# Seven half-size products for the last half of W_o, and a new order of the first loads, in a fused adaLN / linear attention / GEGLU block

## The chip, the cores and the metric

One NeuronCore of one Trainium2 chip. The metric is the device time of one execution in microseconds (us); the kernel before takes 749.21 us (median of 3 runs, 748.36 to 750.71). "TensorE" is the matmul engine (PE in the profile), "VectorE" DVE, "ScalarE" ACT, "GpSimd" POOL, and "the queue of transfers" is SyncE's (SP).

## The reference, cut to what matters

```python
# S = 2048 rows, D = 1024, F = 3584, 32 heads of 32; all inputs bf16
def _A_ref(x, wqkv, wo):                      # linear attention
    ...
    o = num / den
    return (lambda x, *d: x.transpose(*d))(o, 0, 2, 1, 3).reshape(B, S, D) @ wo
def _B_ref(x, w_gate, w_up, w_down):
    return _gelu(x @ w_gate) * (x @ w_up) @ w_down
mod = (_silu(c) @ w_mod).reshape(c.shape[0], 6, 1, -1)
sa, ca, ga, sb, cb, gb = ...
h = _layernorm(x, axis=-1) * (1 + ca) + sa
x = x + ga * _A_ref(h, A_wqkv, A_wo)
h = _layernorm(x, axis=-1) * (1 + cb) + sb
x = x + gb * _B_ref(h, B_w_gate, B_w_up, B_w_down)
```

The kernel folds the attention state into W_o (W' = KV · W_o · ga), so that the W_o stage is one product of 2048 x 1024 by 1024 x 1024. The other large products (Q, K, V, gate, up, down) already use seven half-size products in place of eight (Strassen's scheme, in Winograd's form).

## The kernel before: what the change and the argument touch

Every operation is recorded in a plan. A list scheduler then sets the order of the instructions of VectorE, ScalarE, GpSimd and the queue of transfers from modelled times; TensorE keeps the order of the program. So any change of the program lets the scheduler reorder the other four queues in all of the kernel.

```python
    def order(self):                      # (cut)
        best = None
        def forward(look):
            nonlocal best
            t = self.sweep(False, lambda o: (o.due, o.n), look)
            if best is None or t < best[0]:
                best = (t, sorted((op.start, op.n) for op in self.ops))
        ...
        return [self.ops[n] for _, n in best[1]]
```

```python
    def wo_tile(tt, banks):               # one of 16 tiles of 128 rows: 16 matmuls of 512 columns
        b, tl = tt // TT, tt % TT
        xt = x2_ring()
        ...
        for half in range(NHD):
            for g in range(KD):
                te.matmul(psw[:, half, :], lhsT=pqT[b][:, g, tl * P:(tl + 1) * P],
                          rhs=Wp[:, g, half * NW:(half + 1) * NW], start=(g == 0), stop=(g == KD - 1))
        tt_op(xt, psw.rearrange("p h n -> p (h n)"), xt, ALU.add)
        sy.dma_start(out=x2_scr[b][tl * P:(tl + 1) * P, :], in_=xt)

    xh2_ring = Ring(199, [D], F16, 3)     # three slots for the normalised rows on their way to DRAM

    def ln2_xhat(tt, x2, mv, rstd, op0=ALU.subtract):
        xh = xh2_ring()
        ve.tensor_scalar(out=xh, in0=x2, scalar1=mv[:, 0:1], scalar2=rstd[:, 0:1], op0=op0, op1=ALU.mult)
        sy.dma_start(out=xh_scr[g][h][tl * P:(tl + 1) * P, :], in_=xh)
        if tl == TT - 1:
            h2_load(g, h)                 # transposed load of four tiles: the rows of gate/up

    def wo_phase(ms2):
        for tt in range(NTT):             # 16 tiles
            ...
            if tt == NTT - 2:
                ms2.spread(2, gbrow, 1.0)
            if tt < 2 * TT:               # statistics of the first eight tiles, ScalarE or VectorE
                ...
```

The first eight tiles (row blocks 0 and 1) feed the first gate/up stage through normalisation, a store, a transposed load, modulation ("h2_mod") and differences ("h2_t1" and so on). Row blocks 2 and 3 are normalised later.

Terms used below: PSUM is the memory that matmuls write into; SBUF holds the other tiles. The "spread" is two matmuls that copy the gate row of the modulation to all partitions, and the "shift row" is another row of the modulation, wanted at the start. The "denominators" ("den") are the divisors of the attention; they come back from DRAM in the W_o stage. A "seed copy" is a copy by ScalarE from one PSUM bank to another in gate/up, on which TensorE then goes on adding. Names such as s1, s2, t1 or t2 are sums of sub-blocks (s of rows, t of weights) that the seven products take as operands.

## Time and profile before

| | before |
|---|---|
| time, median | 749.21 us |
| span of the profiled run | 746.4 us |
| TensorE busy | 730.0 us, 98% |
| W_o stage, first tile after the denominators to gate/up | 194.75 to 245.6 us |
| VectorE busy from 195 to 250 us | 39.03 of 55 us |
| first gate/up stage | 245.6 to 414.5 us |

The profile is one execution. A group line gives start, length, engine, source line, operation, operands and count; a bracket gives the idle time of the engine just before and what ended it. The prediction shows the summary, the chain, VectorE at three spots and the start. One view more, TensorE in the first gate/up stage (244 to 420 us): these are all its lines with an idle time.

```profile
321.99 4.48 PE L1382 MATMUL psum<-mem 128*128 128x512 f16 x20 [0.31 <-ACT psum L1436]
358.61 4.48 PE L1382 MATMUL psum<-mem 128*128 128x512 f16 x20 [0.16 <-ACT psum L1436]
381.88 0.38 PE L1393 MATMUL psum<-mem 128*128 128x256 f16 x2 [0.42 <-DVE psum L564]
```

Together 0.9 us in 169.

### The profile page before, as it was taken

How to read it: one execution, taken by the hardware profiler on the slowest of the kernel's cores; microseconds unless marked ns; L12 is line 12 of the kernel's file. 1: busy time of each engine (PE TensorE's matmuls, PEld its weight loads, DVE VectorE, ACT ScalarE, POOL GpSimd, SP SyncE). 2: the span in 40 equal slices, each digit the busy share in tenths (PEclk: the TensorE clock that was granted, in tenths of full speed). 3: DMA queues.
4: the chain of work that ended last, by engine and by line, in shares of the span. 5: the costliest groups of instructions: out<-in, count | busy, mean ns of one | idle time of the engine just before them, and what ended most of it. 6: DMA issues, size and time to landing. Idle time of an engine off the chain costs nothing.

```text
span 746.4 us, 11439 instructions
## 1 busy us (share of the span) xinstructions
PE 730.0 (98%) x4164; PEld 388.7 (52%) x4164; DVE 589.5 (79%) x1258; ACT 433.0 (58%) x757; POOL 95.8 (13%) x164
## 2 busy tenths in 40 slices
PE   5999999999999999999999999999999999999997
PEld 2444445444444455545454586545555555548664
DVE  6897997577786878777997888678888888888763
ACT  3665576669752768997876234027777777731000
POOL 2331245000001113342311000010000000000000
PEclk9999999999999999999999999999999999999999
DMA  8974479828899979899659799654131322399822
GB/s 298 322 212 132 152 182 163 299 101 258 245 290 257 364 253 261 259 318 227 187 191 237 210 281 314 206 183 132 60 114 57 112 73 98 110 276 302 278 104 71
DMA packets 151832, 152.79 MB, mean 205 GB/s; under 512 B 33824, under 2 KB 128544, under 8 KB 150496
## 3 DMA queue, kind: packets, MB, share of 16 engines
q1 hardware_dynamic: 128832, 122.44, 53.7%
q0 software_dynamic: 20592, 27.53, 15.6%
q10 hardware_dynamic: 2352, 2.10, 0.8%
q8 instruction: 32, 0.52, 0.3%
q14 instruction: 24, 0.20, 0.1%
HBM read 123.34 MB, written 36.04 MB: 214 GB/s over the span
## 4 chain that ended last, share of the span: by engine, by line
PE 84%; DVE 6%; ACT 5%; DMA 3%; issue 1%; SPq 1%; ACTq 0%; DVEq 0%
PE psum L1382 30%; PE psum L1588 13%; PE psum L1632 9%; PE psum L870 8%; PE psum L1393 7%; PE psum L1262 7%; PE psum L940 5%; DVE mem L564 5%; PE psum L969 4%; DMA mem<-in_A_wqkv_dram 2%; DMA mem<-in_w_mod_dram 1%; PE psum L984 1%; ACT mem L815 1%; DVE psum L564 1%; ACT psum L1436 1%
## 5 line engine op out<-in xcount | busy, mean ns | idle before, releaser
L564 DVE TENSOR_TENSOR mem<-mem 128x512 f16<-128x512 f16 (+8 forms) x669 | 307.8, 507 | 23.1 <-ACT mem L815 10.1
L1382 PE MATMUL psum<-mem 128*128 128x512 f16 x1248 | 299.1, 379 | 0.8 <-ACT psum L1436 0.5
L815 ACT ACTIVATE mem<-psum 128x256 f32<-128x256 f32 (+3 forms) x284 | 154.3, 562 | 119.9 <-PE psum L1382 45.1
L564 DVE TENSOR_TENSOR mem<-psum,mem 128x512 f16<-128x512 f32 (+4 forms) x204 | 155.4, 767 | 72.8 <-ACT mem L815 29.5
L1382 PEld LDWEIGHTS <-mem 128*128 128x128 f16 (+1 forms) x1248 | 122.0, 98 | 112.1 <-issue 2.7
L1588 PE MATMUL psum<-mem 128*128 128x512 f16 (+2 forms) x462 | 99.2, 373 | 0.5 <-DVE mem L564 0.5
L1393 PE MATMUL psum<-mem 128*128 128x256 f16 x560 | 89.5, 272 | 1.3 <-DVE psum L564 1.2
L1393 PEld LDWEIGHTS <-mem 128*128 128x128 f16 (+1 forms) x560 | 54.7, 98 | 46.8 <-issue 5.1
L1588 PEld LDWEIGHTS <-mem 128*128 128x128 f16 x462 | 45.2, 98 | 49.8 <-issue 0.7
L1632 PE MATMUL psum<-mem 128*128 128x256 f16 (+1 forms) x588 | 66.2, 273 | 0.0
L870 PE MATMUL psum<-mem 128*128 128x512 f16 (+1 forms) x280 | 62.9, 379 | 0.0
L1632 PEld LDWEIGHTS <-mem 128*128 128x128 f16 x588 | 57.5, 98 | 9.2
L1436 ACT ACTIVATE psum<-psum 128x512 f32<-128x512 f32 x56 | 32.8, 587 | 41.3 <-PE psum L1382 28.9
L1262 PE MATMUL psum<-mem 128*128 128x512 f16 x256 | 56.0, 379 | 0.0
L940 PE MATMUL psum<-mem 128*128 128x512 f16 x224 | 51.2, 379 | 0.0
L564 DVE TENSOR_TENSOR psum<-psum,mem 128x256 f32<-128x256 f32 x80 | 34.3, 429 | 17.7 <-ACT mem L815 17.3
L870 PEld LDWEIGHTS <-mem 128*128 128x128 f16 x280 | 26.9, 97 | 31.8 <-DVE mem L789 1.2
L1262 PEld LDWEIGHTS <-mem 128*128 128x128 bf16 x256 | 24.8, 98 | 30.3 <-issue 0.8
L1453 ACT ACTIVATE mem<-psum 128x512 f16<-128x512 f32 x56 | 33.1, 595 | 10.9 <-PE psum L1382 10.5
L1463 ACT ACTIVATE mem<-mem 128x512 f16<-128x512 f16 x56 | 34.9, 625 | 1.5 <-DVE mem L564 1.1
L940 PEld LDWEIGHTS <-mem 128*128 128x128 f16 (+1 forms) x224 | 21.5, 98 | 27.0 <-issue 2.0
L1049 POOL DMA_DIRECT2D ts<-in_B_w_down_dram x28 | 28.3, 1199 | 9.2 <-DMA ts<-in_B_w_down_dram 8.9
(132 smaller groups left out, 525.3 us busy)
## 6 DMA issues: line engine op xcount, KB each, us to landing
mem<-in_B_w_gate_dram SPq DMA_DIRECT2D x14, 1024.0 KB, 7.0
mem<-in_B_w_up_dram SPq DMA_DIRECT2D x14, 1024.0 KB, 5.4
mem<-in_w_mod_dram SPq DMA_DIRECT2D x24, 512.0 KB, 5.9
mem<-ts SPq DMA_DIRECT2D x6, 1792.0 KB, 6.8
mem<-in_A_x_dram SPq DMA_DIRECT2D x32, 256.0 KB, 7.7
ts<-in_B_w_down_dram POOLq DMA_DIRECT2D x28, 256.0 KB, 6.3
mem<-ub SPq DMA_DIRECT2D x16, 448.0 KB, 6.7
mem<-in_B_w_down_dram SPq DMA_DIRECT2D x12, 448.0 KB, 7.8
```

The costliest lines, as they stand in the source:

```text
L564: ve.tensor_tensor(out=out, in0=a, in1=b, op=op)
L815: ac.activation(out=t, in_=ps, func=AF.Copy)
L870: te.matmul(ps, lhsT=A[:, k, i * P:(i + 1) * P], rhs=B[:, k, :], start=(start and k == 0), stop=(k == KH - 1), skip_group_check=True)
L940: te.matmul(o, lhsT=W[:, k, (j0 + i) * P:(j0 + i + 1) * P], rhs=h_form(a, k), start=(start and k == 0), stop=(k == KH - 1), skip_group_che ...
L1262: te.matmul(psw[:, half, :], lhsT=pqT[b][:, g, tl * P:(tl + 1) * P], rhs=Wp[:, g, half * NW:(half + 1) * NW], start=(g == 0), stop=(g == K ...
L1382: te.matmul(ps, lhsT=a[:, k, e, :], rhs=b[:, k, :], start=(start and k == 0), stop=(k == KH - 1), skip_group_check=True)
L1393: te.matmul(ps, lhsT=self.x[a][:, k, :], rhs=self.y[y][:, k, :], start=(start and k == 0), stop=(k == KH // 2 - 1), skip_group_check=True)
L1436: ac.activation(out=z, in_=x, func=AF.Copy)
L1453: ac.activation(out=o, in_=ps, func=AF.Gelu_apprx_tanh)
L1463: ac.activation(out=o, in_=o, func=AF.Gelu_apprx_tanh)
L1588: te.matmul(psm[:, q, c], lhsT=A[:, i, q * P:(q + 1) * P], rhs=wt[:, i, c], start=(start and i == 0), stop=(i == NPR - 1), skip_group_chec ...
L1632: te.matmul(ps[:, q, :], lhsT=a[:, k, q * P:(q + 1) * P], rhs=y[:, k, :], start=(start and q == 0 and k == 0), stop=(k == NPR // 2 - 1), s ...
```

## The change

Its intent: W_o of row blocks 2 and 3 costs seven half-size products a block in place of eight (112 matmuls for 128), with the sums of W' and of the rows made on VectorE meanwhile. At the start, the first loads come in the order in which the first products want them, W_v in quarters, so that the first V product can begin sooner.

```diff
+    WpT = [at(11.75 + 4 * i, [KH, NW], F16) for i in range(4)]
+    x2_pair = [at(o, [2, D], BF16) for o in (191, 195, 176, 180)]
...
+    START_LOADS = "c a0 x0 a1 x1 a2 a3 v0 x2 v1 x3 v2".split()
...
-        load_w(Wv[:, 0:KH, 0:NW], 2 * D, NW, 0, KH)
-        load_w(Wv[:, KH:KD, 0:NW], 2 * D, NW, KH, KD)
-        load_w(Wv[:, :, NW:D], 2 * D + NW, NW)
-        plan.chain.append(plan.ops[-1])
+        for name, c in (("v0", slice(0, HB)), ("v1", slice(HB, NW)), ("v2", slice(NW, D))):
+            load_w(Wv[:, :, c], 2 * D + c.start, c.stop - c.start)
+            loads[name] = plan.ops[-1]
+        plan.chain += [loads[name] for name in START_LOADS]
...
-            xh.append(ln_rows(x))
+            xh.append(ln_rows(x, i in (2,3,)))          # statistics of two tiles on ScalarE
...
-        for tt in range(NTT):
+        for tt in range(2 * TT):                        # eight tiles only
...
             if tt == 2:
                 den_sums(1, psX())
+                for i in range(4):
+                    wp_sum(i)
             if tt == 6:
                 ms2.columns()
                 ve.tensor_scalar_add(out=opcB, in0=modT[:, 4 * KD:5 * KD], scalar1=1.0)
+                ms2.spread(2, gbrow, 1.0)
...
+            if tt == 2 * TT - 1:
+                for b in (2, 3):
+                    for i in range(4):
+                        h_sum(b, i, pqT)
+                stages = {2: wo_stages(2, QC, QD)}
+                stages[2][0]()                          # product (2,1), ahead of tile 7
...
+    ORDER = ((2, 3), (2, 2), (3, 1), (2, 5), (3, 3), (2, 4), (3, 2), (2, 6), (3, 5), (2, 7), (3, 4), (3, 6), (3, 7))
+    def wo_stages(b, A, B):
+        ...
+        def s1():
+            st["a"] = products(A.pair(), "a11", "b11", True)
+            st["c"] = B.pair()
+            ac.activation(out=st["c"], in_=st["a"], func=AF.Copy)
+        def s3():
+            st["u2"] = fcopy(lambda: u2 if b == 2 else p1, products(st["a"], "s2", "t2", False))
```

Product (b, j) is number j of row block b. The change also edits some hints to the scheduler (how early the loads of the denominators and the transposed loads are placed).

## The prediction

> **What bounds the kernel now.** I read the engine summary first, then the chain of work that ended last, then the stretches of the two places that the change touches: the first 36 us, and the product with W_o from 195 to 250 us.
>
> ```profile
> PE 730.0 (98%) x4164; PEld 388.7 (52%) x4164; DVE 589.5 (79%) x1258; ACT 433.0 (58%) x757; POOL 95.8 (13%) x164
> ...
> PE 84%; DVE 6%; ACT 5%; DMA 3%; issue 1%; SPq 1%; ACTq 0%; DVEq 0%
> ```
>
> TensorE is busy in 730.0 of 746.4 us and carries 84% of the chain. So a matmul taken away is worth its own time, provided that no new wait opens beside it. The chain, in order of time, in the W_o stage:
>
> ```profile
> 194.81 7.01 PE psum L1262 x32
> ...
> 210.68 0.08 PE psum L592 x4
> 210.76 31.10 PE psum L1262 x144
> 241.86 0.43 PE psum L600 x2
> 242.29 3.45 PE psum L1262 x16
> 245.75 8.63 PE psum L1382 x40
> ```
>
> L1262 is the product with W_o, L600 the spread of the gate row, L1382 the gate/up stage. 31.10 / 144 gives 0.216 us a matmul with 512 columns, and the stages follow each other with no gap. VectorE is not idle here, though:
>
> ```profile
> 195.00:250.00 55.00, 55.00 (x283) 24.86 (x282) 39.03 (x60) 29.34 (x58) 1.87 (x3) 1.00 1.00 277
> ```
>
> After the length come PE, PEld, DVE, ACT and POOL: DVE 39.03 of 55 us. The timeline of VectorE at three spots of this stage:
>
> ```profile
> 197.41 2.50 DVE L564 TENSOR_TENSOR mem<-mem 128x1024 bf16<-128x1024 bf16 x4 [2.12 <-DMA mem<-den]
> 199.82 1.22 DVE L564 TENSOR_TENSOR mem<-psum,mem 128x1024 bf16<-128x1024 f32 x1
> ...
> 216.47 0.17 DVE L594 COPY mem<-psum 128x16 f32<-128x16 f32 x1
> ...
> 244.15 1.39 DVE L564 TENSOR_TENSOR mem<-mem 128x1024 f16<-128x1024 f16 x2 [3.40 <-ACT mem L1240]
> 245.79 1.23 DVE L564 TENSOR_TENSOR mem<-psum,mem 128x1024 bf16<-128x1024 f32 x1 [0.24 <-PE psum L1262]
> ```
>
> The first two lines give the prices: 1024 elements from SBUF 0.63 us each (2.50 / 4), a W_o tile added out of PSUM 1.22 (1.14 from start to start). The pair at 244.15 makes h2_t1, the first difference that gate/up needs; it is done 1.8 us before gate/up's ninth matmul wants it (245.6 + 8 x 0.216 = 247.3). At the start:
>
> ```profile
> 26.50 0.83 PE L636 MATMUL psum<-mem 128*32 128x512 bf16 x12
> 28.07 0.40 PE L636 MATMUL psum<-mem 128*32 128x512 bf16 x4 [0.73 <-DMA mem<-in_w_mod_dram]
> 28.40 0.82 PE L691 MATMUL psum<-mem 128*128 128x512 f16 x3
> ...
> 12.00:19.00 7.00, 5.72 (x34) 2.16 (x32) 3.98 (x13) 1.58 (x4) 0.00 (x0) 1.00 1.09 359
> 20.00:26.00 6.00, 6.00 (x30) 2.70 (x29) 5.37 (x15) 2.65 (x5) 2.24 (x6) 1.00 1.05 385
> ```
>
> TensorE has done all that precedes the shift row of the modulation (L636) by 27.3 us and waits for the last quarter of that row's weights until 28.07. The last two numbers of the stretches say why: the 16 DMA engines are full (1.09, 1.05), at 359 and 385 GB/s. The start is bound by bytes, not by the order of the first products.
>
> [...] ScalarE stood 13.5 us behind the spread of L600 while later work was ready. My two stalls below rest on it. [...] W_v in quarters has rows of exactly 512 B. No run before shows that size.
>
> **The change, part by part.** *Matmuls removed.* Row blocks 2 and 3 took 8 tiles x 16 = 128 matmuls. Seven products take 2 blocks x 7 x 2 row halves x 4 = 112. Gain 16 x 0.216 = 3.45 us. The instruction count of TensorE stays at 4164: two W_v tiles at the start are now made in column halves, 32 matmuls of 256 for 16 of 512, the same column time. So it can't be read from the count.
>
> *Work added, VectorE.* Four sums of W' of 2048 elements (about 1.16 us each, an estimate from the 0.63 us pieces: 4.6), eight row sums of 1024 (8 x 0.60 = 4.8), four second adds of the outputs (2.4). The adds out of PSUM stay at four a block. Together 11.8 us: DVE goes from 39 of 55 to about 51 of 52. ScalarE gets six copies of 1024 (about 1.0 each), 35 of 52: room. Sums of rows, and the division by the denominator ahead of them, are done in time by my count (the second sum of block 3 at about 227, where its product starts at 226.8).
>
> *A stall at the spread.* In the order of the built program the gate row's spread moved from before the last W_o tile to before tile 6. Its second matmul writes the bank that VectorE's 16-column copy (L594 above) reads, so TensorE must wait for that copy. VectorE's queue ahead of it, from the landing of block 1's denominators at 197.4: four multiplies 2.4, tiles 0 and 2 2.3, two W' sums 2.3, tile 3 1.1, a W' sum 1.2, row copy 0.6, two normalisations 0.9, statistics 1.2, tile 4 1.1, a statistic and a normalisation 0.6, two multiplies 1.3, the copy 0.2: 15.2 us, so 212.6. TensorE is there at 210.97. That is 1.7 us if the denominators land when they did. Fewer bytes stand ahead of them in the new order of loads, so they may land 1 to 3 us sooner and the stall may go. I take 0.8.
>
> *A stall at gate/up.* Call T the end of the last W_o product. Before, h2_t1 was placed ahead of the last tile's add. In the changed program VectorE's queue has the last product's add first, then a small sum, three modulations, then h2_t1. From T: [...] 1.14 the add, 0.3, 3 x 0.365, 0.6 for the first half: T + 3.25. TensorE has eight matmuls without it (T + 1.73), so it waits 1.5 us, and about 0.2 more for the second half, whose modulation ScalarE makes after the seed copy (T + 3.0, sum at T + 3.8). I take 1.7. After that VectorE is ahead again.
>
> *The start.* Both orders put the same 8.4 MB (x, W_v, two modulation rows, the next x tiles) ahead of the last shift-row quarter. So the quarter lands when it did, whatever the first products do: opcA about 1.4 us sooner (0.5 MB less ahead of it), first V matmul near 14.1 instead of 15.03, all of it waiting again at 28. The two 512 B quarters may cost bytes per second: 359 at 1 KB rows and 385 at 2 KB rows fit about 6 ns a row plus 39.5 ns per KB on each of 16 engines; 512 B would then run near 316 GB/s, 1.05 MB in 3.3 instead of 2.9 us, +0.4. Interleaving large loads with the small x loads may fill the thin stretch from 2 to 6 us (244 GB/s) and give as much back. Net 0.
>
> Sum: -3.45 + 0.8 + 1.7 + 0 = -0.95; 749.21 - 0.95 = 748.3.
>
> **The rivals.** (a) The full saving, 745.8: TensorE is 98% busy and the chain holds nothing else in this stage. Against it: VectorE has 1 us of slack left in 52, and its order puts h2_t1 behind an add that can't start before T. (b) VectorE becomes the bound of the whole W_o stage; a load that waits behind it (the denominators, the transposed rows) makes it worse; 750 to 751. For it: 51 of 52. Against it: it waits for products anyway from 230 on. The second transposed load, issued at about 228, lands near 239 with the 10 us that the former needed, some 4 us before VectorE asks. (c) The start pays too, 1 us from the earlier first product: 747.3, with (a) 744.8. Against it stands the wait at 28.07. (d) The scheduler reshuffles VectorE and ScalarE everywhere: TensorE's order is the same elsewhere and it waits little there; +-0.7 us.
>
> **Range and chances.** Each stall may be 0 to 2.5 us, the start -0.8 to +0.8, the reshuffle +-0.7. All for the better gives about 744.5, all for the worse 751.5; 745.6 to 750.4 should hold 8 times in 10. Two per cent are 15 us, more than four times the matmuls removed: within 2% 0.98, 0.01 on either side.
>
> **What would show it.** In the changed trace: 16 matmuls fewer between the two stages at 0.216; an idle time of TensorE at the second spread matmul near 211, ended by VectorE (0 to 2 us); one after eight gate/up matmuls, ended by VectorE, of 1.5 to 2; TensorE waiting for the last shift-row quarter at 27.6 to 28.6. I am wrong if gate/up runs through its first 40 matmuls as before, if the last quarter lands more than 1 us sooner, or if new waits show in stages that the change does not touch.

Cut from it: one term of 0.1 us in the stall at gate/up, for the step from the last product's end to VectorE's start, which the trace does not show: before, the add started at 245.79, 0.04 us after the modelled end of the product at 245.75. T + 3.25 counts that term; without it the terms come to T + 3.14 and that wait to 1.4 us in place of 1.5. The forecast was made with it, and its sum stays: -3.45 + 0.8 + 1.7 + 0 = -0.95. That an operation of ScalarE or VectorE holds up what stands behind it in its queue is my reading of the one case named there: ScalarE was idle for 13.49 us before the copy at 242.33, and the modulation behind that copy began only at 243.30, though its rows had been there since 237.8 by the trace's landing records.

## The result, and the profile after

| | before | after |
|---|---|---|
| median of 6 runs | 748.91 us (747.8 to 750.71) | 752.82 us (750.66 to 753.33) |
| ratio | | 1.0046, 95% interval 1.0029 to 1.0063 |
| profiled run | 746.4 us span | 748.9 us span, the fastest of its six |

A ratio here is always the mean time of one kernel's fast runs over that of the other's of the same rounds, so not quite the ratio of the medians.

The change loses 3.4 us by the means (3.9 by the medians); predicted was 748.3 (745.6 to 750.4), a gain of 0.95. Within 2% the two kernels are the same, as predicted. The summary of the page and the shares of the chain after:

```profile
PE 728.4 (97%) x4150; PEld 389.1 (52%) x4164; DVE 600.3 (80%) x1277; ACT 442.1 (59%) x771; POOL 102.1 (14%) x164
...
PE 76%; DMA 6%; DVE 6%; ACT 5%; SPq 3%; issue 2%; DVEq 0%; ACTq 0%
```

TensorE's share of the chain fell from 84% to 76%; that of transfers doubled, from 3% to 6%. In order of time, the chain now runs through other engines in the middle of the W_o stage:

```profile
206.76 7.08 DMA xhs<-mem
...
215.63 1.29 DVE mem L571 x2
...
217.00 1.14 DVE mem L571
218.16 1.16 ACT mem L1223 x2
...
221.14 0.92 ACT psum L1410
...
222.11 7.08 PE psum L901 x32
```

Read it backwards. TensorE's product (2,3), L901, started at 222.11, when ScalarE's copy of product (2,1), L1410, was done. That copy's input had been ready since 216.3, but it stood in ScalarE's queue behind the statistics of tile 6 (L1223, L1224), which waited for VectorE's sum of tile 6 (L571 at 217.00). VectorE was late because at 213.97 it had waited for a *store*: with three slots for normalised rows, tile 3's row could not be written before tile 0's had left, and that store (xhs) took 7 us beside the loads of the denominators. The lines of TensorE from 190 to 258 us that have an idle time:

```profile
210.77 0.38 PE L607 MATMUL psum<-mem 128*128 128x512 f16 x1 [0.94 <-DVE mem L601]
222.11 20.88 PE L901 MATMUL psum<-mem 128*128 128x512 f16 x96 [2.33 <-ACT psum L1410]
243.22 1.89 PE L901 MATMUL psum<-mem 128*128 128x512 f16 x8 [0.23 <-DVE mem L571]
248.66 7.24 PE L1490 MATMUL psum<-mem 128*128 128x512 f16 x32 [1.83 <-DVE mem L571]
```

The first and the last are the two stalls that I predicted (0.8 and 1.7). The second I had not seen. VectorE in this stretch, with its wait for the store, and then the busy times from 195 to 250 us, the window that the prediction shows for the kernel before:

```profile
213.97 1.14 DVE L1232 TENSOR_SCALAR mem<-mem 128x1024 f16<-128x1024 bf16 x2 [2.12 <-DMA xhs<-mem]
...
216.91 1.22 DVE L571 TENSOR_TENSOR mem<-psum,mem 128x1024 bf16<-128x1024 f32 x1
```

```profile
195.00:250.00 55.00, 49.67 (x255) 22.01 (x253) 48.54 (x72) 33.77 (x64) 2.48 (x3) 1.00 0.98 265
```

VectorE is busy 48.54 of 55 us, 9.5 more than before, TensorE 5.3 us less. The start answers to the lines shown before like this:

```profile
14.35 3.07 PE L703 MATMUL psum<-mem 128*128 128x256 f16 x16 [0.58 <-DVE mem L693]
...
27.36 1.05 PE L641 MATMUL psum<-mem 128*32 128x512 bf16 x16
28.34 1.04 PE L703 MATMUL psum<-mem 128*128 128x512 f16 x4
```

V began at 14.35 instead of 15.03, but after the shift row's 16 matmuls (L641) it goes on at 28.34, against 28.40 before, and K begins at 31.91 against 31.96: nothing is left of it. In this run TensorE did not wait for the last quarter of that row's weights. It came to it only at 27.36, since the first half-width V products ran slowly (3.07 us for what takes 16 x 0.109 = 1.7 at full clock: their starts are 0.20 to 0.21 us apart until the trace grants the full clock at 16.8 us, in the kernel before at 12.3, and 0.109 after it).

The quarters of W_v with rows of 512 bytes did come more slowly. Between 11 and 14 us nearly all packets are theirs (1654 packets for 0.89 MB, 538 bytes on average):

```profile
11.00:14.00 3.00, 2.52 (x18) 1.48 (x18) 1.19 (x3) 2.02 (x3) 0.00 (x0) 1.00 1.19 298
```

That is 298 GB/s (last column) at full transfer engines, where the kernel before moved 377 in the same window. From 2 to 6 us it is the other way round, 299 against 244, and over the first 36 us the two are level, 328 against 321.

**An account that adds up.** Both kernels run the same matmuls in the same order from gate/up on, so their weight loads can be matched one by one. This table is worked out from the start times in the traces: how much later than in the kernel before (+) each kernel's matmul is, in us.

| matmul | time before | changed kernel | start_only | wo_only | before_tail_after | wo_slots_late_180 |
|---|---|---|---|---|---|---|
| first of gate/up | 245.37 | -0.64 | -0.11 | -1.66 | +3.11 | -3.80 |
| its 41st | 254.00 | +1.51 | -0.11 | -1.42 | +3.11 | -3.57 |
| first of down | 414.54 | +3.07 | +4.51 | +3.54 | +5.24 | -2.00 |
| first of second gate/up | 494.99 | +3.56 | +4.51 | +3.54 | +6.24 | -2.00 |
| first of second down | 661.43 | +2.49 | +4.63 | +2.64 | +5.04 | -2.03 |
| last | 742.59 | +2.48 | +4.62 | +2.63 | +5.03 | -2.04 |

(The other columns are experiments, below.) For the changed kernel: W_o's third tile already came 1.17 sooner (193.58 for 194.75). To gate/up: -1.17 - 3.45 (16 matmuls) + 0.94 + 2.33 + 0.23 makes -1.12; measured -0.64, so half a microsecond lies in steps too small for the idle column. Then the 1.83 stall and more small steps. Then **+1.56 in the first gate/up stage, +0.49 in down, -1.07 in the second gate/up: stages that the change does not touch.**

What costs 1.56 where the idle column of the changed kernel shows 0.20? In the trace, five weight loads come 0.471 us after the one before in the changed kernel that come after 0.216 or 0.248 in the kernel before. One of the spots, ScalarE, first after and then before:

```profile
274.56 0.60 ACT L1561 ACTIVATE mem<-psum 128x512 f16<-128x512 f32 x1 [1.34 <-PE psum L1490]
275.05 0.59 ACT L1544 ACTIVATE psum<-psum 128x512 f32<-128x512 f32 x1
```

```profile
273.04 0.58 ACT L1436 ACTIVATE psum<-psum 128x512 f32<-128x512 f32 x1 [1.56 <-PE psum L1393]
```

The PSUM copy that TensorE needs next (L1544, before L1436) now stands behind an activation (L1561) that no engine is seen to wait for here. TensorE gets it 0.255 us too late. The modelled end of a matmul hides most of the gap: its record lasts 0.379 us on average, where starts are 0.216 apart.

### The profile page after: what moved, and what is told of

It is laid out like the page before. It is cut to its first block, busy times and chain, and to the rows that moved or that the text cites. A ratio compares the mean times of both kernels' runs of the same rounds, so it can differ in the third digit from the quotient of the medians.

```text
span 748.9 us, 11458 instructions
## 1 busy us (share of the span) xinstructions
PE 728.4 (97%) x4150; PEld 389.1 (52%) x4164; DVE 600.3 (80%) x1277; ACT 442.1 (59%) x771; POOL 102.1 (14%) x164
## 4 chain that ended last, share of the span: by engine, by line
PE 76%; DMA 6%; DVE 6%; ACT 5%; SPq 3%; issue 2%; DVEq 0%; ACTq 0%
PE psum L1490 29%; PE psum L1696 12%; PE psum L901 9%; PE psum L1740 7%; PE psum L1501 7%; DVE mem L571 5%; PE psum L971 4%; PE psum L1000 4%; DMA mem<-den 3%; PE psum L703 2%; SPq L1217 2%; ACT mem L845 1%; DMA mem<-in_w_mod_dram 1%; PE psum L1015 1%; ACT psum L1544 1%
## 5 line engine op out<-in xcount | busy, mean ns | idle before, releaser
L571 DVE TENSOR_TENSOR mem<-mem 128x1024 f16<-128x1024 bf16 (+13 forms) x685 | 321.5, 515 | 19.7 <-ACT mem L845 9.0
L1490 PE MATMUL psum<-mem 128*128 128x512 f16 x1248 | 300.5, 379 | 3.0 <-DVE mem L571 1.8
L845 ACT ACTIVATE mem<-psum 128x256 f32<-128x256 f32 (+3 forms) x286 | 156.9, 567 | 115.9 <-PE psum L1490 44.3
L571 DVE TENSOR_TENSOR mem<-psum,mem 128x512 f16<-128x512 f32 (+4 forms) x204 | 155.2, 767 | 70.6 <-ACT mem L845 29.8
L1490 PEld LDWEIGHTS <-mem 128*128 128x128 f16 (+1 forms) x1248 | 122.0, 98 | 116.0 <-issue 7.3
L901 PE MATMUL psum<-mem 128*128 128x512 f16 (+1 forms) x384 | 86.3, 379 | 2.9 <-ACT psum L1410 2.3
L1501 PEld LDWEIGHTS <-mem 128*128 128x128 f16 (+1 forms) x560 | 54.7, 98 | 45.6 <-issue 3.8
L1696 PEld LDWEIGHTS <-mem 128*128 128x128 f16 x462 | 45.2, 98 | 49.9 <-issue 0.7
L1740 PEld LDWEIGHTS <-mem 128*128 128x128 f16 x588 | 57.5, 98 | 9.8 <-DMA mem<-ts 0.8
L901 PEld LDWEIGHTS <-mem 128*128 128x128 f16 (+1 forms) x392 | 38.0, 98 | 47.3 <-issue 2.1
L1544 ACT ACTIVATE psum<-psum 128x512 f32<-128x512 f32 x56 | 33.1, 591 | 44.3 <-PE psum L1490 34.9
L971 PE MATMUL psum<-mem 128*128 128x512 f16 x224 | 51.2, 379 | 0.0
L571 DVE TENSOR_TENSOR psum<-psum,mem 128x256 f32<-128x256 f32 x80 | 34.3, 429 | 15.3 <-ACT mem L845 14.9
L1561 ACT ACTIVATE mem<-psum 128x512 f16<-128x512 f32 x56 | 33.3, 596 | 17.0 <-PE psum L1490 16.7
L971 PEld LDWEIGHTS <-mem 128*128 128x128 f16 (+1 forms) x224 | 21.5, 98 | 27.1 <-issue 2.4
L1000 PE MATMUL psum<-mem 128*128 128x512 bf16 x126 | 28.7, 379 | 0.1
L1293 PE MATMUL psum<-mem 128*128 128x512 f16 x128 | 28.5, 379 | 0.0
```

The source lines that it names most:

```text
L571: ve.tensor_tensor(out=out, in0=a, in1=b, op=op)
L845: ac.activation(out=t, in_=ps, func=AF.Copy)
L901: te.matmul(ps, lhsT=A[:, k, i * P:(i + 1) * P], rhs=B[:, k, :], start=(start and k == 0), stop=(k == KH - 1), skip_group_check=True)
L971: te.matmul(o, lhsT=W[:, k, (j0 + i) * P:(j0 + i + 1) * P], rhs=h_form(a, k), start=(start and k == 0), stop=(k == KH - 1), skip_group_che ...
L1000: te.matmul(ps, lhsT=hr1[b][:, k, tl * P:(tl + 1) * P], rhs=Wk[:, k, n * NW:(n + 1) * NW], start=(k == 0), stop=(k == KD - 1))
L1490: te.matmul(ps, lhsT=a[:, k, e, :], rhs=b[:, k, :], start=(start and k == 0), stop=(k == KH - 1), skip_group_check=True)
```

## The experiments

Eighteen runs, each five rounds beside the kernel before. Two theories stood at first: **W**, the loss is made in the W_o stage by waits; **T**, the scheduler's new order of untouched stages makes it. And for the wait of 2.33 us: **A**, ScalarE's queue order, against **B**, VectorE's backlog. A rival to all was that the start part costs.

| run | median, us | before, us | ratio, 95% interval | mean clock 0.998 or less |
|---|---|---|---|---|
| start_only | 753.0 | 748.73 | 1.0052 (1.0037 to 1.0067) | 5 of 6 runs |
| wo_only | 750.81 | 748.73 | 1.0025 (1.0013 to 1.0037) | 3 of 5 |
| s1_copy_first | 750.91 | 748.73 | 1.0034 (1.0019 to 1.0049) | 1 of 6 |
| store_slots | 749.23 | 748.73 | 1.0007 (0.9994 to 1.0021) | 1 of 6 |
| start_tail_before | 749.42 | 750.14 | 1.0003 (0.9986 to 1.0019) | 1 of 6 |
| after_tail_before | 754.88 | 750.14 | 1.0066 (1.0053 to 1.0079) | 6 of 6 |
| before_tail_after | 754.68 | 750.14 | 1.0069 (1.005 to 1.0087) | 4 of 6 |
| slots_t1_tail | 751.92 | 750.14 | 1.0041 (1.0015 to 1.0067) | 6 of 6 |
| after_late | 752.0 | 748.71 | 1.0046 (1.0034 to 1.0058) | 5 of 6 |
| slots_t1 | 749.54 | 748.71 | 1.0017 (1.0001 to 1.0032) | 1 of 6 |
| slots_t1_late | 748.99 | 748.71 | 1.0001 (0.9988 to 1.0014) | 0 of 5 |
| all_late | 750.14 | 748.71 | 1.0016 (1.0 to 1.0033) | 0 of 6 |
| stores_first_late | 747.91 | 748.67 | 0.9986 (0.997 to 1.0003) | 0 of 5 |
| wo_late_60 | 749.86 | 748.67 | 1.0009 (0.999 to 1.0029) | 2 of 6 |
| wo_late_120 | 747.36 | 748.67 | 0.9981 (0.9964 to 0.9999) | 0 of 5 |
| wo_slots_late | 746.96 | 748.67 | 0.997 (0.9951 to 0.9989) | 0 of 5 |
| wo_slots_late_180 | 746.31 | 749.51 | 0.9957 (0.9944 to 0.9971) | 0 of 5 |
| wo_slots_late_240 | 747.38 | 749.51 | 0.998 (0.9961 to 1.0) | 2 of 6 |

All gave correct results. The intervals are 0.9 to 2 us either way, so what lies below that rests on the traces, not on the times. A trace is one execution: differences of a few tenths between two traces show something only where they recur.

### Each half of the change alone

start_only is the kernel before with the start hunks of the change; wo_only is the changed kernel with those hunks taken back:

```diff
 # start_only
-        ca = ModRow(1, wm_ca, {0: loads[0], 2: loads[1], 4: loads[2], 6: loads[3]})
-        load_w(Wv[:, 0:KH, 0:NW], 2 * D, NW, 0, KH)
+        ca = ModRow(1, wm_ca)
+        for name, c in (("v0", slice(0, HB)), ("v1", slice(HB, NW)), ("v2", slice(NW, D))):
 # ... the rest of the start as in the change; wo_only is the reverse, with wo_phase as changed
```

> The kernel before with the start part alone (order of the first loads, W_v in quarters, statistics of two tiles on ScalarE, column halves of the first V products); W_o stays at eight products. Theory 1, the start gives nothing: the last shift-row quarter still sets TensorE near 28.1 us, the first K product comes within 0.3 us of 31.96, and the whole is the kernel before plus or minus 0.7 us of reshuffled order, 748.2 to 749.6. Rival, the start is what costs (512 B rows, ScalarE's statistics): K starts 1 us later or more and the kernel is 750.5 or above. Second rival, the start hides a gain: 747.5 or below.

> The changed kernel with the start of the kernel before; the seven products of W_o stay. Theory 1: the whole loss is made in and after the W_o stage, so this one is as slow as the changed kernel within 1 us (751.5 to 753.5; ratio to the kernel before 1.003 to 1.006), with a wait of TensorE of about 2 us before product (2,3) and one of 1.5 to 2 us after eight gate/up matmuls. Rival, the start part is half of the loss: 749.5 to 750.7.

start_only lost most: 753.0, above the rival's bound. But not in the start: K began at 31.82 (before 31.96), and gate/up at -0.11. It lost it at 405 us, in one wait of TensorE:

```profile
405.46 0.38 PE L1409 MATMUL psum<-mem 128*128 128x256 f16 x2 [3.64 <-DVE psum L564]
```

VectorE's lines tell why:

```profile
403.17 0.69 DVE L1582 TENSOR_TENSOR mem<-mem 128x1024 f16<-128x1024 f16 x1 [4.18 <-DMA xhs<-mem]
...
404.98 0.43 DVE L564 TENSOR_TENSOR psum<-psum,mem 128x256 f32<-128x256 f32 x1
```

The scheduler had put an operation that waits 4.18 us for a transfer (a store of normalised rows, xhs) ahead of the PSUM sum (404.98) that TensorE needs. And the wait cost a second time (columns: busy times of PE, PEld, DVE, ACT, POOL, then the granted clock, the share of the transfer engines, GB/s):

```profile
395.00:401.00 6.00, 6.00 (x33) 3.10 (x32) 3.95 (x7) 4.02 (x8) 0.00 (x0) 1.00 1.03 208
406.00:409.00 3.00, 3.00 (x10) 1.22 (x8) 2.32 (x4) 1.94 (x4) 0.00 (x0) 0.50 0.68 221
```

After the wait the clock was 0.50: 10 matmuls in 3 us where 33 fitted in 6. The trace has one such spell of 3.413 us, from 406.02. The mean clock of this run is 0.998, and such a spell costs up to 1.7 us (half of 3.4, at clock 0.50; an estimate from these numbers); the last column of the table counts runs with so low a mean clock. A mean clock of 0.998 does not by itself show a wait like this one: the kernel before, whose trace has no wait of 1 us after the first 20 us, has 9 of them in its 55 runs beside the experiments, and in wo_only's trace (mean clock 0.998) the spell lies in the start (15.29 to 18.70 us).

wo_only reached gate/up 1.66 us *ahead* of the kernel before, with waits of 0.33 (spread) and 0.80 (product (3,3)) and none after eight gate/up matmuls. It then lost 5.2 us inside gate/up, 1.68 of it at 303 us in a wait for VectorE, the rest in steps of 0.2 to 0.5. So theory W is wrong as a whole: the seven products alone pay at their own place, and each half of the change, with an order of its own, loses in the same untouched stage. My number for wo_only (751.5 to 753.5) missed by 0.7, and the two waits of about 2 us that I expected with it did not come.

### The wait of 2.33 us: ScalarE's order or VectorE's backlog

Both runs keep every queue's order of the changed kernel; one moves a single instruction in the finished order, the other adds slots.

```diff
 # s1_copy_first: in the finished order, ops go right behind "to"
+            for ops, to in self.moves:
+                for op in ops:
+                    seq.remove(op)
+                i = seq.index(to)
+                seq[i + 1:i + 1] = ops
+    plan.moves.append(([tag["copy", 2]], eng(tag["stage", 2, 1], "PE")[-1]))
 # store_slots
     xh2_ring = Ring(199, [D], F16, 3)
+    xh2_ring.slots += Ring(184, [D], F16, 3).slots
```

> The changed kernel with exactly one instruction of ScalarE moved: the PSUM copy of the first product of block 2 stands ahead of tile 6's statistics instead of behind them; all other orders are the changed kernel's. Theory A, ScalarE's queue order is the cause of the 2.33 us: the wait before product (2,3) goes and with it 2.3 us, about 750.5. Theory B, VectorE is 2 us behind in this stage whatever ScalarE does: product (2,3) then waits for VectorE's row sum s2 of block 2 (ready at 220.4 in the changed kernel's trace, so a wait of about 0.7) and product (3,3) for s2 of block 3 (ready at 228.7, wanted at 227.4, a wait of about 1.4); (3,3) starts within 0.4 us of where it did (229.0) and the time changes by 0.5 us or less, about 752.4.

> The changed kernel with six slots instead of three for the normalised rows of W_o's tiles, so that VectorE's normalisation of tile 3 no longer waits for the store of tile 0; the order of every queue is the changed kernel's. Theory B (VectorE's backlog, begun by that 2.12 us wait, is what sets the stage): VectorE is 2.1 us ahead from 214 on, tile 6's sum ends near 216, ScalarE's copy near 220, product (2,3) waits 0.2 instead of 2.33 and (3,3) comes 2 us sooner: about 750.6. Theory A (only ScalarE's queue order) gives the same here, so it is the pair with s1_copy_first that tells them apart. Rival C: the wait is hidden anyway, since VectorE then waits for the denominators or for TensorE instead: less than 0.7 us gained.

TensorE in s1_copy_first:

```profile
220.61 7.08 PE L909 MATMUL psum<-mem 128*128 128x512 f16 x32 [0.72 <-DVE mem L579]
229.40 15.71 PE L909 MATMUL psum<-mem 128*128 128x512 f16 x72 [1.71 <-DVE mem L579]
```

Theory B: 0.7 and 1.4 were expected, 0.72 and 1.71 came, both for VectorE, and (3,3) began at 229.40, no sooner than in the changed kernel (229.01). (The move brought the copy behind the first of the four statistics instructions, not ahead of all, so my text overstated it; it still ended at 220.39 instead of 222.06.) In the trace the end moved by 0.46 us. The median, 750.91, is 1.9 under the changed kernel's and near what theory A expected (750.5), but the intervals of the two ratios overlap, and one of its six runs has a low mean clock against three; so I go by the trace. In store_slots the wait is gone and nothing took its place up to gate/up:

```profile
220.95 22.77 PE L911 MATMUL psum<-mem 128*128 128x512 f16 x104
```

104 matmuls in one piece; the stall after eight gate/up matmuls stayed, 1.82 us. Against the changed kernel the 41st gate/up matmul came 1.4 us sooner (+0.12 for +1.51), although the denominators had landed 1.1 us later in this run (and the wait at the spread was 1.38 for 0.94); the end of the trace came 1.17 us sooner, and the ratio fell from 1.0046 to 1.0007, which is more than the trace explains. So the cause of the 2.33 us is the three-slot buffer, two engines upstream of the one that the profile names, in this order of the queues: wo_only has three slots too, VectorE waits 1.14 us for a store there, and product (2,3) does not wait.

### The order of the untouched stages, transplanted

The instructions from the first gate/up stage on are the same in both kernels, so one kernel's order of each queue can be given to the other. The point from which the given order holds is called the seam below; here it is the first instruction of gate/up:

```diff
-            for op in self.order():
+            seq = self.tail_as(self.order(), TAIL)   # TAIL: for each queue, the order of the
+            for op in seq:                           # instructions recorded from gate_up(0) on
```

> The run start_only, with one thing more: from the first gate/up stage on, the instructions of VectorE, ScalarE, GpSimd and of the queue of transfers are issued in the order that they had in the kernel before (the operations are the same; only the scheduler had reordered them). Theory T, the loss of start_only (753.0) is the reordering of the gate/up stage, which in its trace made a wait of 3.64 us for VectorE at 405 us followed by 3.4 us of half clock: this run is then the kernel before within 0.7 us, 748.0 to 749.2. Rival, the start part itself costs (or leaves something behind that costs later): 751 or more.

> The changed kernel, with the order of the kernel before from the first gate/up stage on; start and W_o stage as in the changed kernel. Theory T: the 1.6 us lost between the 40th gate/up matmul and the first down matmul, and 0.5 in the first down stage, go; the 1.0 us that the changed order gained in the second gate/up stage goes too. What stays are the waits of the W_o stage and of the first gate/up matmuls: 1.5 us over the kernel before, 750.4, and fewer runs with a lowered clock. Rival, the gate/up stage is late because its rows are late, in any order: 752 or more, with the same steps of 0.26 us in its trace.

> The kernel before with the changed kernel's order from the first gate/up stage on, nothing else. Theory T: it loses 1.6 us in the first gate/up stage and 0.5 in the first down stage and wins 1.0 in the second gate/up stage, as the changed kernel did: 749.8 (749.3 to 751, more if half-clock spells come). Rival, the order is harmless without the late rows: 748.2 to 749.2.

> The changed kernel with the order of the kernel before from gate/up on, six slots for the normalised rows (as in store_slots) and the three modulations and h2_t1 placed ahead of the last product's sum in VectorE's queue, two of ScalarE's modulations ahead of its seed copy. If my account adds up: no wait before (2,3) (-2.3 us against the changed kernel), the stall of 1.8 us after eight gate/up matmuls falls to 0.1 to 0.7, the reordering is undone: 1 to 1.5 us under the kernel before, 747.2 to 747.9. Rival: VectorE is the bound of this stretch, the work moved behind makes TensorE wait a few products later, and the time stays at 749 to 750.

start_tail_before: 1.0003 instead of 1.0052, and its trace ends 0.60 us *under* the kernel before. The start part does not cost, and gives at most that much. In this run the full clock came early (12 us; the two 512-column matmuls at 12.23 took 0.59 us, the two at 12.62 in the changed kernel 1.06) and TensorE did wait for the last shift-row quarter, as in the kernel before:

```profile
27.84 0.40 PE L680 MATMUL psum<-mem 128*32 128x512 bf16 x4 [0.50 <-DMA mem<-in_w_mod_dram]
```

It lands at 27.84 for 28.07. Theory T for this half is shown.

before_tail_after is the kernel before with nothing changed but this order: 1.0069. Its column in the account: +3.11 at the seam (a wait of 3.29 us for VectorE before the last W_o tile, since the transplanted order suits another W_o stage), then +2.13 to down, +1.00 in down, -1.20 in the second gate/up: the same signs as in the changed kernel, where it was +1.56, +0.49 and -1.07. The five steps from 0.216 or 0.248 to 0.471 us recur here at the very same matmuls (0.471 or 0.472). The order itself does it, with or without W_o's change. My number (749.3 to 751) missed by 3.7 us, nearly all of it the wait at the seam.

after_tail_before missed my 750.4 by 4.5 us, and not because the steps stayed: from its 41st gate/up matmul (+6.42) to its end (+6.37) it is flat. The seam broke instead, with 4.92 us of TensorE waiting for VectorE until 252.21 and a spell of half clock from 251.91 to 255.33. slots_t1_tail broke in the same way (3.79 us at 249.47, with two spells in a row, mean clock 0.995) and missed its 747.9 by 4 us. So in the next runs the seam came later.

### A later seam, and the stall at gate/up

From the 120th gate/up matmul on (some 26 us into the stage) the order is the earlier one. "t1" puts h2_t1 ahead of the last product's sum:

```diff
+    plan.n0 = len(plan.ops) + 207                    # "late": the seam 120 matmuls after gate_up(0) begins
 # t1
+    plan.moves.append((eng(tag["stage", 3, 7], "DVE")[:1], tag["fill", 7][1]))
+    plan.moves.append(([seed], tag["fill", 5][3]))   # ScalarE: two modulations ahead of the seed copy
 # all_late has besides: spread behind tile 6, (2,1)'s copy sooner, row sum s2 of block 3 before an output sum
+    plan.moves.append((tag["spread"], tag["tile", 6]))
```

> The changed kernel; from the 120th matmul of the first gate/up stage on (some 26 us into it, so that the seam with W_o is left alone, which after_tail_before broke) every engine's order is that of the kernel before. Theory T: against the changed kernel's trace, the steps of 0.26 us in the first gate/up stage and the 0.5 us of the first down stage go (-1.8 us from there to the second gate/up stage) and the 1.0 us won in the second gate/up stage goes too, so the sum is only about 1 us: end of the trace at 1.5 us over the kernel before, ratio 1.002 to 1.004. Rival: the steps stay, ratio 1.0045 or more.

> store_slots plus one thing: in VectorE's queue three modulations and h2_t1 ahead of the sum of the last W_o product, in ScalarE's queue two modulations ahead of the first seed copy; all else in the changed kernel's order. If the last product's sum ahead of h2_t1 is the cause of the stall after eight gate/up matmuls (1.82 us in store_slots), it falls to 0.1 to 0.7 and the kernel is 1.1 to 1.7 us under store_slots, ratio to the kernel before 0.998 to 1.000. Rival: the transposed rows land too late for it (in slots_t1_tail, which has this too, the wait was 3.79 us), the stall stays 1.5 us or grows.

> slots_t1 and after_late in one. If the three causes add (2.3 us of VectorE's wait for a store, 1.8 us of the last sum ahead of h2_t1, about 1 us net of the reordered gate/up stage): 1 to 1.5 us under the kernel before, ratio 0.998 to 0.9987. Rival: one of them only moves on, ratio 0.9995 or more.

> slots_t1_late with the spread of the gate row after tile 6 instead of before it (the 0.9 to 1.4 us wait for VectorE's copy of 16 columns goes), ScalarE's first copy of block 2 ahead of tile 6's statistics, and VectorE's second row sum of block 3 ahead of its first output sum. If VectorE keeps up: up to 1.3 us under slots_t1_late, 2 to 2.5 us under the kernel before, ratio 0.9967 to 0.998. Rival: VectorE is the bound there, TensorE waits at product (3,3) for the row sum instead, and it equals slots_t1_late within 0.4 us.

after_late: the same ratio as the changed kernel, 1.0046, above what I expected. Its trace shows theory T's part: flat at +3.3 from 295 us to the end. But a wait of 1.06 us stands at the new seam, and the old wait before (2,3), here 2.54 us, was followed by a spell of half clock (222.02 to 225.44). And the 1.07 us that the new order wins in the second gate/up stage had gone with the rest.

slots_t1 (1.0017) and slots_t1_late (1.0001) both missed what I expected, by 0.0017 and 0.0014. They say that my explanation of the stall after eight gate/up matmuls was half the truth. VectorE in slots_t1_late:

```profile
243.77 1.06 DVE L1331 TENSOR_SCALAR mem<-mem 128x512 f16<-128x512 f16 x3 [0.43 <-DMA mem<-xhs]
244.74 1.28 DVE L625 TENSOR_TENSOR mem<-mem 128x1024 f16<-128x1024 f16 x2
245.94 1.22 DVE L625 TENSOR_TENSOR mem<-psum,mem 128x1024 f16<-128x1024 f32 x1
```

The sum (245.94) is now behind h2_t1 (244.74), as wanted, and TensorE still waited 1.22 + 0.60 us (in both runs): the modulations (243.77) could not begin before the transposed rows had landed. all_late, expected at 0.9967 to 0.998, removed the wait at the spread (0.50 us in slots_t1_late) and gained only 0.28 us at the end of the trace: TensorE came sooner and waited 0.67 instead of 0.28 just ahead of gate/up, then 1.16 + 0.60 for the same rows. Its time, 1.0016, can't be told from slots_t1_late's by the intervals.

```diff
 # stores_first_late = slots_t1_late and
+    plan.moves.append(([tag["x", 2, 1], tag["x", 3, 0]], xh2_stores[7]))   # two loads of x behind the last store
```

> slots_t1_late with two loads of x (512 KB each) moved behind the last store of normalised rows in the queue of transfers. In slots_t1_late that store was issued at 226.8 and landed near 234.4, and the transposed load that needs it came in at 243.7, just when VectorE wanted it. If that landing is what holds the stall after eight gate/up matmuls at 1.22 + 0.60 us: the store lands 3 us or more sooner, the transposed rows with it, the two waits fall to 0.6 or less together, and the kernel is 1 us or more under slots_t1_late. Rival: the stall is VectorE's and ScalarE's own modulations and sums, and stays at 1.5 to 1.8; or the store lands as late, since the 16 engines of transfers are full.

The transposed load was issued at 230.57 instead of 234.48, its rows were there 1.2 us sooner, and the waits fell from 1.22 + 0.60 to 0.90 + 0.60:

```profile
244.29 2.06 PE L1561 MATMUL psum<-mem 128*128 128x512 f16 x8 [0.90 <-DVE mem L625]
246.95 5.51 PE L1561 MATMUL psum<-mem 128*128 128x512 f16 x24 [0.60 <-DVE mem L625]
```

The end came 1.2 us sooner (-0.52 for +0.69), ratio 0.9986. So the landing was the bound, as claimed; that the waits would fall to 0.6 was wrong, since TensorE also came to gate/up 0.9 us sooner, and the load itself took longer (9.94 us in the queue instead of 7.22). That the transfer engines were full is so in slots_t1_late's trace: from 222 to 245 us the packets of one queue took 104.9% of the time of the 16 engines, and all together moved 302 GB/s.

### The seven products alone, in the earlier order

> wo_only (seven products, start of the kernel before) with the order of the kernel before from the 60th gate/up matmul on. Theory T: it reaches gate/up 1.5 to 2 us ahead of the kernel before, as wo_only did, and keeps it: ratio 0.9975 to 0.9985. Rival: gate/up needs what W_o's stage makes too late, in any order, and eats it: ratio 1.000 or more.

> The same from the 120th matmul on. Theory T: ratio 0.9975 to 0.999, with perhaps a wait of 1 us at the seam near 273 us, as slots_t1_late had, and the steps of 0.26 us before the seam.

> wo_late_120 with six slots for the normalised rows, so that VectorE's wait of 1.14 us for a store and TensorE's of 0.80 before product (3,3) go. If VectorE's backlog is what that wait was: 0.5 to 1 us under wo_late_120. Rival: hidden by the denominators or by the transposed load: the same within 0.3 us.

> wo_slots_late with the seam 60 matmuls later. If the 1.06 us wait is the seam's: it is gone from 272 us (perhaps another stands near 285), one more step of 0.26 us of the new order is paid, ratio 0.996 to 0.9975. If it is late work of VectorE: it stays at 272, ratio 0.997.

> The same with the seam 120 matmuls later: if the wait was the seam's it is gone from 272 us, and up to four steps of 0.26 us of the new order are paid instead, ratio 0.9965 to 0.998.

```diff
 # all five: the start of the kernel before, seven products, the earlier order from a later seam;
 # the three "slots" runs: six slots for normalised rows
+    plan.n0 = len(plan.ops) + 111 / 207 / 313 / 409  # seam after 60 / 120 / 180 / 240 gate/up matmuls
```

wo_late_120 gave 0.9981, as expected. wo_late_60 gave 1.0009, the rival's number, but its seam costs two waits, 1.17 and 1.30 us. The 1.06 us wait at 271.6 moved with the seam, to 282.5 (0.81) at 180 and 293.9 (0.95) at 240: it is the seam's. wo_slots_late_240 gave 0.998, as expected; wo_slots_late_180, expected at 0.996 to 0.9975, is the best, 746.31 us, ratio 0.9957, all five runs at full clock (mean clock 1.0) and within 0.45 us. Its W_o stage and the first gate/up matmuls:

```profile
219.34 22.61 PE L939 MATMUL psum<-mem 128*128 128x512 f16 x104
241.78 9.03 PE L1545 MATMUL psum<-mem 128*128 128x512 f16 x40
```

Gate/up began at 241.78 instead of 245.6 and ran through its first 40 matmuls without a wait. **So the seven products pay once a buffer is deep enough and the tuned order of the next stage is kept: 3.2 us in the times (749.51 to 746.31; 2.2 to 4.2 by the interval), 2.04 us at the end of the trace.** Two reservations. Of the 3.80 us at gate/up, 1.42 were there at the third W_o tile already (193.33 for 194.75), so they are not the products'. And this seam is the best of three, picked afterwards: at 120, 180 and 240 the ratios are 0.997, 0.9957 and 0.998. wo_slots_late's profiled run was its slowest (748.28) and had a late start, with the full clock granted only from 21 us on (its first 16 V products took 6.16 us, for 4.17 in wo_slots_late_180); its table entry, not that trace, is what to compare; by it the deeper buffer gave 0.0011 in the ratio, within the intervals, so not shown here.

## Why the prediction was wrong, point by point

- **16 matmuls fewer, -3.45: right to about half a microsecond.** From the third W_o tile to gate/up, waits taken off, the stage is 2.97 us shorter in the changed kernel, 2.89 in store_slots and 3.06 in wo_slots_late_180.
- **Stall at the spread, +0.8: right**, 0.94 in the changed kernel, none (after_late) to 1.61 (slots_t1_tail) in the variants that kept its place, depending on when the denominators landed and when TensorE came: in these three traces VectorE's first multiply by them came at 195.65, 194.72 and 197.16.
- **Stall at gate/up, +1.7: right in size (1.83), half right in cause.** I had "the second transposed load ... lands near 239 ... some 4 us before VectorE asks". It was issued only at 237.01 and held the queue of transfers until 244.18, because a load of x ahead of it in that queue had waited 5.7 us for a store (x2s) to free its buffer. That is a wait for a store once more, and I had not followed that queue either. With the sum moved away (slots_t1_late) the landing held TensorE as long.
- **Start, 0: right**, start_tail_before can't be told from the kernel before. The mechanism, the last shift-row quarter, shows in that run (a wait of 0.50 us until 27.84); in the changed kernel's own trace TensorE was late for it by its clock, a case that I had not thought of. Both halves of the guess about bytes came true: the 512-byte rows ran at 298 GB/s (I had 316), and the thin stretch from 2 to 6 us filled up (299 for 244).
- **"Sums of rows, and the division by the denominator ahead of them, are done in time by my count": the step that failed in the W_o stage.** I compared totals (51 of 52 us of VectorE) and one spot (s2 of block 3). The total was not the trouble: VectorE's busy time grew by 9.5 us where I had counted 11.8. I did not follow the queue with its waits, so I missed the store that a three-slot buffer makes VectorE wait for (2.12), and the chain from there over ScalarE's queue to product (2,3): +2.33, and 0.23 later. The nearest is my rival (b), VectorE as the bound, but it spoke of loads that wait behind VectorE, not of a store that VectorE waits for. store_slots shows the cause: with six slots this wait is gone.
- **"The scheduler reshuffles ... +-0.7": the term that was too narrow.** I argued from TensorE's order, which stays, and from its waiting little. In the changed kernel's trace the later stages cost 0.98 net (+1.56, +0.49, -1.07), a little outside my range. How wide the term really is shows in the other programs: from gate/up to the end 4.73 us in start_only (with the spell), 4.29 in wo_only, and 1.92 in before_tail_after, where nothing else was changed (its 1.0069 holds the wait at the seam too). My "new waits ... in stages that the change does not touch" came as steps that the idle column does not show. The kernel before is the outcome of tuning, so its order is a good one among many, and all three programs that the scheduler ordered anew lost in the first gate/up stage.
- **The sum.** Forecast was -0.95, the trace has +2.48. Of the 3.43 us between them, the two unforeseen waits are 2.56, the reordered later stages 0.98, small steps 0.80 and the two stalls 0.27; W_o's third tile came 1.17 sooner. The worst case was also added up wrongly: by my own terms it is 752.3, not 751.5 (and the best 744.3, not 744.5).
- **A cost that had no term:** half clock after a wait; in start_only's trace 3.4 us of it followed the wait of 3.64. Three of the changed kernel's six runs have the mean clock of one spell (0.998) and took 752.67 to 753.11; its profiled run had none, which is why the trace shows 2.5 us of loss and the median 3.9. That the spells of those runs follow the 2.33 us wait is possible (after_late's did, behind the same wait) but not shown: only profiled runs have traces, and a spell can lie in the start as well, as wo_only's did. One run of 753.33 us at a mean clock of 1.0 stays unexplained.

## What to carry to other kernels

Where a scheduler orders the queues, a change anywhere is a change everywhere: price the reorder by transplanting the order alone, with the seam well away from the stage that changed (three of the four transplants with the seam right at gate/up made a wait of 3.29 to 4.92 us there), and keep the tuned order of the stages that you do not touch. When an engine nears the time of its stage, don't compare sums of busy time; walk its queue with every wait that it meets, above all waits for a buffer that a store has to free. And follow a wait to its source before mending it: here ScalarE was named, moving its copy gave 0.46 us in the trace, and three more slots two engines upstream freed it.
